# Sums of two weight matrices made by copying and accumulating DMAs instead of on VectorE

## The chip, the cores and the metric

The kernel runs on one core of a Trainium2 chip. The metric is device time in microseconds (us). The core has TensorE (PE in the profile; PEld is its weight load), VectorE (DVE), ScalarE (ACT), GpSimd (POOL) and SyncE (SP, which here only issues DMAs; its rows are written SPq). The profile counts the packets of all DMA queues on one set of 16 DMA engines; the busy share that it gives for them sums the packets' times, so it can pass 1. The granted clock is the share of full speed that the chip allowed PE. Each kernel was timed against the kernel before on the same chip.

## The reference, cut to what matters

```
x = A_x                                     # 2048 x 1024, bf16
g = sigmoid((x * gate_w).sum(-1))
a = attention(x @ wqkv) @ wo                # sliding window of 8, dilation 2, 32 heads
b = (gelu(x @ w_gate) * (x @ w_up)) @ w_down   # 1024 -> 3584 -> 1024
return g * a + (1 - g) * b
```

The last products of both branches, `... @ wo` (1024 x 1024) and `... @ w_down` (3584 x 1024), run in one accumulation, which the text below calls the down products.

## The kernel before: the parts that matter

The big products are done with seven block products in place of eight, which need sums of weight blocks. For the down products these are four sums T1 to T4 of the blocks B11, B12, B21, B22 of w_down and of wo. The sums are the same for all four chunks of 512 rows of x, so the kernel makes them once, keeps them in DRAM (`ddram`, `odram`) and loads them for every chunk.

The kernel is emitted by a small planner. Streams of operations are merged by planned time, and each engine gets its instructions in that order. What the planner believes of a DMA is this:

```python
# Weave._emit
if op.eng in ("SP", "POOL"):
    nbytes, issue = op.cost
    self.clk[op.eng] = t + issue
    self.pipe = max(self.pipe, t) + nbytes / self.RATE      # RATE = 340e3 bytes per us
    op.end = self.pipe + 2.2
```

Every engine executes strictly in the order that the planner chose. If a DMA takes longer than planned, what stands behind a wait for it on that engine is late too.

The sums before the change: SyncE loads blocks of the weights, VectorE subtracts, GpSimd stores.

```python
def preps():
    for i0 in range(0, NPREP, 2):                 # 9 groups
        ...
        f0 = dve(t, lambda: V(out=fo[:, 0], in0=b12, in1=b11, op=ALU.subtract), [("prep", i0)], lag=1.0)
        ...  # fo2 = b22 - b12,  fo1 = b22 - fo0,  fo3 = b21 - fo1
        for f in range(4):
            o = Op("POOL", (n * P * NW * 2, 0.8),
                   lambda f=f: nc.gpsimd.dma_start(out=dd[:, f, r0:r0 + n, :], in_=fo[:, f]), [last], ...)
            yield o
```

The first FFN (`ffn(0)`) has sums too, of the gate and up weights. VectorE makes them in a ring of 20 buffers, and GpSimd stores them for the second FFN. A ring buffer comes free when the matmuls have read it and its store has landed:

```python
# wforms: 56 stores
yield Op("POOL", (P * GR * 2, 0.6),
         lambda b=b, f=f: nc.gpsimd.dma_start(out=fdram[b][:, f * GR:(f + 1) * GR],
                                              in_=ring[:, held[("w", 0, b, f)], :]),
         [("w", 0, b, f)], key=("ws", b, f))
# ffn, after the last matmul that reads the sum
ring_give(("w", sup, b, form), o, w.done[("ws", b, form)])
```

SyncE loads the weight blocks into that ring. In the same queue, beside blocks 9 to 12, it loads the other half of x with transposing DMAs, in four groups of four:

```python
for b in range(2, NBLK):
    yield from load_block(0, b)
    if b >= XB:                                   # XB = 9
        for c, k0 in ((2, 0), (2, 4), (3, 0), (3, 4))[b - XB:b - XB + 1]:
            yield from list(load_x(c, []))[k0:k0 + 4]
```

Of the kernel before, what the change touches and what calls it, by code (L numbers as in the profile page):

```python
# [14 lines left out]
P = 128  # L15
# [15 lines left out]
class Op:  # L31


    def __init__(self, eng, cost, fn, deps=(), key=None, table=None, pre=None, lag=0.0, tail=0.08, kind=None):
        self.eng, self.cost, self.fn, self.deps, self.key = eng, cost, fn, deps, key
        self.table, self.pre, self.lag, self.tail = table, pre, lag, tail
        self.kind = kind
        self.end = None


class Weave:
# [42 lines left out]
    def _emit(self, op, t):  # L84
        cost = op.cost
        if op.eng == "ACT" and op.table is not None and op.table != self.table:
            self.table = op.table
            cost += 1.29
# [3 lines that stand above are left out]
            self.pipe = max(self.pipe, t) + nbytes / self.RATE  # L92
            op.end = self.pipe + 2.2
        else:
            self.clk[op.eng] = t + cost
            op.end = t + cost + op.tail
        instructions = self.nc.cur_bb.bb.instructions
        n0 = len(instructions)
        op.fn()
        for ins in self.nc.cur_bb.bb.instructions[n0:]:  # L100
            eng = getattr(ins, "engine", None)
            if eng is None or not getattr(ins, "name", None) or type(ins).__name__.startswith("BassTile"):
                continue
            prev = self.last.get(eng)
            if prev is not None:
                self.tc.add_manual_dep(ins, prev, mybir.DependencyInfo(mybir.DependencyClass.NoSync,
                                                                      mybir.DependencyReason.DATA),
                                       reason="engine order")
            self.last[eng] = ins.name
            self.names.append((ins.name, len(self.log)))  # L110
        if op.key is not None:
            self.done[op.key] = op
        self.log.append((op.eng, t, op.end, op.key, op.fn.__qualname__.split(".")[2], op.cost))
# [23 lines left out]
def kernel(  # L137
# [156 lines left out]
    w.pipe = 6.0  # L294

    vbuf = hT[:, :, 0:NT, :].rearrange("p k f n -> p k (f n)")
    NPREP = FH + NTH
    def stage(i):
        f0 = 8 + 4 * i
        return hT[:, :, f0:f0 + 4, :].rearrange("p (a b) f s -> p a b (f s)", b=2)  # L300

    def qkv_src(which, k0, n):
        return A_wqkv[k0 * P:(k0 + n) * P, which * D:(which + 1) * D].rearrange("(k p) n -> p k n", p=P)

# [5 lines left out]
    def load_x(c, deps):  # L310
        deps = deps + ([[("acct", 1)], [("att", 0)]][c - 2] if c > 1 else [])
        for kt in range(KT):
            yield Op("SP", (P * SC * 2, 1.6), lambda kt=kt: nc.sync.dma_start_transpose(
                out=xT(c, kt), in_=x[c * SC:(c + 1) * SC, kt * P:(kt + 1) * P]), deps, key=("x", c, kt))

    def load_prep(i0):
        n = min(2, NPREP - i0)
        kind, src, nr = ("d", B_w_down, FH) if i0 < FH else ("o", A_wo, NTH)
        r0 = i0 if kind == "d" else i0 - FH
        si = i0 % 5  # L320

        def fn():
            st = stage(si)
            for h, r in ((0, r0), (1, nr + r0)):
                if kind == "d":
                    v = src[r * P:(r + n) * P, :].rearrange("(k p) (h n) -> p k h n", p=P, h=2)
                else:
                    v = AP(src.tensor, src.offset + r * D, [[NT * D, P], [D, n], [NW, 2], [1, NW]])
                for k in range(n):
                    nc.sync.dma_start(out=st[:, 2 * h + k], in_=v[:, k])  # L330
        return Op("SP", (4 * n * P * NW * 2, 2.0 * n), fn, [("preps", i0 - 6)] if i0 >= 6 else [], key=("prep", i0))

    def load_block(sup, b):
        c0, c1 = b * FB * P, (b + 1) * FB * P
# [30 lines left out]

    def loads():
        yield from load_qkv(0, 0)
        yield load_prep(0)
        yield from load_qkv(0, 1)
        yield Op("SP", (KT * P * D * 2, 1.0), lambda: [nc.sync.dma_start(out=vbuf[:, hf * KH:(hf + 1) * KH],  # L370
                                                                        in_=qkv_src(2, hf * KH, KH)) for hf in range(2)],
                 [("pt", NST - 1, 1)], key=("wqkv", 0, 2))
        yield load_prep(2)
        yield from load_x(1, [])
        for i0 in (4, 6, 8, 10):
            yield load_prep(i0)
        yield from load_block(0, 0)
        yield load_prep(12)
        yield from load_block(0, 1)
        for i0 in (14, 16):  # L380
            yield load_prep(i0)
        for b in range(2, NBLK):
            yield from load_block(0, b)
            if b >= XB:
# [15 lines left out]
                yield from load_down(c0 + 1)  # L400

    def preps():
        for i0 in range(0, NPREP, 2):
            kind, r0, n = ("d", i0, min(2, FH - i0)) if i0 < FH else ("o", i0 - FH, min(2, NPREP - i0))
            st, ot = stage(i0 % 5), stage((i0 + 1) % 5)
            b11, b12, b21, b22 = st[:, 0:n, 0], st[:, 0:n, 1], st[:, 2:2 + n, 0], st[:, 2:2 + n, 1]
            fo = ot[:, :, 0:n, :]
            t = tt(n * NW)
            f0 = dve(t, lambda: V(out=fo[:, 0], in0=b12, in1=b11, op=ALU.subtract), [("prep", i0)], lag=1.0)
            yield f0  # L410
            yield dve(t, lambda: V(out=fo[:, 2], in0=b22, in1=b12, op=ALU.subtract))
            f1 = dve(t, lambda: V(out=fo[:, 1], in0=b22, in1=fo[:, 0], op=ALU.subtract), [f0])
            yield f1
            last = dve(t, lambda: V(out=fo[:, 3], in0=b21, in1=fo[:, 1], op=ALU.subtract), [f1])
            yield last
            dd = (ddram if kind == "d" else odram)[:].rearrange("f p (k n) -> p f k n", n=NW)
            for f in range(4):
                o = Op("POOL", (n * P * NW * 2, 0.8),
                       lambda f=f: nc.gpsimd.dma_start(out=dd[:, f, r0:r0 + n, :], in_=fo[:, f]), [last],
                       key=("preps", i0) if f == 3 else None)  # L420
                yield o
            if i0 + 2 == FH:
                w.done[("stored", "d")] = o
            if i0 + 2 == NPREP:
                w.done[("stored", "o")] = o

    def wforms():
        t = tt(GR)
# [280 lines left out]
    def gate(c):  # L709
# [18 lines left out]
                key=("zq", c))  # L728
        yield e
        ez = small.tile([P, SC // 32], F32, tag="ez", bufs=2, name="ez")  # L730
        omg = small.tile([P, NST], F32, tag="omg", bufs=3, name="omg")
        gates[c] = (ez, omg, zq)

    def gate_sum(c):
# [14 lines left out]
    def gate_tail(c):  # L749
        ez, omg, og = gates[c]  # L750

        def tail():
            nc.vector.tensor_scalar(out=og[:], in0=ez[:], scalar1=1.0, scalar2=1.0, op0=ALU.mult, op1=ALU.add)
            nc.vector.reciprocal(out=og[:], in_=og[:])
            for q in range(4):
                nc.vector.tensor_copy(out=omg[32 * q:32 * (q + 1), :],
                                      in_=og[32 * q:32 * (q + 1), :].rearrange("p (j q) -> p j q", q=4)[:, :, q])
        yield dve(1.2, tail, [("ez", c)], lag=0.6, key=("omg", c))

    accs = {}  # L760
# [202 lines left out]
    def ffn(sup, mid, early=()):  # L963
# [29 lines left out]
        for i in range(FT + 2):  # L993
# [33 lines left out]
            if 1 <= i < FT + 1:  # L1027
                f = i - 1
                o = yield from prod(Bk[f], 2, T3, f, False, [ev[f, "u2"]])
                d = [("stored", "o")] if (sup == 0 and f >= 8) else []  # L1030
                if sup and f >= FT - NT:
                    d = [("qkv", 2 * sup + 1, 0, 0)]
                ev[f, "up2"] = dve(tt(SC, True), lambda f=f: nc.vector.tensor_tensor(  # L1033
                    out=hs(f, 1), in0=v3(banks[Bk[f]][:]), in1=v3(m5[f][:]), op=ALU.add), [o, ev[f, "m5"]] + d)
                yield ev[f, "up2"]
# [27 lines left out]
    def down(c):  # L1063
# [31 lines left out]
        def forms():  # L1095
            for g in range(2):
                j2 = 2 * g + 1
                yield form(ops[g]["S1"], quarter(j2, 0), quarter(j2, 1), ALU.add, ("S1", c, g), hdone + [("ffn", sup)])
                yield form(quarter(j2, 0), ops[g]["A11"], quarter(j2, 0), ALU.subtract, ("S3", c, g))
            for g in range(2):  # L1100
                yield form(ops[g]["S2"], ops[g]["S1"], ops[g]["A11"], ALU.subtract, ("S2", c, g), [("pr", c, 0, g)])
# [34 lines left out]
    def down_rest(c, ops, prod, forms, form, ev, A, Bk, Dk, m5, u2, omg):  # L1136
# [18 lines left out]
        for m in range(1, 7):  # L1155
            for g in range(2):
                j1, j2 = 2 * g, 2 * g + 1
                om1, om2 = omg[:, j1:j1 + 1], omg[:, j2:j2 + 1]
                box = []
                if m == 1:  # L1160
                    o = yield from prod(A[g], m, g, False, [ev[g, "seed"]])
                    e = act(0.6, lambda g=g, om1=om1, box=box: scaled(A[g], om1, ost_tile(box)), [o, ("omg", c)])
                    yield from evac(e, j1, 0, box)
                    bank_give(A[g], e)
                    yield form(ops[g]["S4"], ops[g]["A12"], ops[g]["S2"], ALU.subtract, ("S4", c, g), [o])
                elif m == 2:
                    Dk[g], fr = bank_take()
                    o = yield from prod(Dk[g], m, g, True, [fr])
# [14 lines left out]
                elif m == 4:  # L1183
                    o = yield from prod(Bk[g], m, g, False, [ev[g, "u2"]])
                    ev[g, "x"] = dve(0.67, lambda g=g, om2=om2, box=box: nc.vector.scalar_tensor_tensor(
                        out=ost_tile(box), in0=banks[Bk[g]][:], scalar=om2, in1=m5[g][:], op0=ALU.mult, op1=ALU.add),
                        [o, ev[g, "m5"]])
                    yield from evac(ev[g, "x"], j2, 1, box)
                elif m == 5:
                    o = yield from prod(Dk[g], m, g, False, [ev[g, "m5"]])  # L1190
                    e = dve(0.67, lambda g=g, om1=om1, box=box: nc.vector.scalar_tensor_tensor(  # L1191
                        out=ost_tile(box), in0=banks[Dk[g]][:], scalar=om1, in1=u2[g][:], op0=ALU.mult, op1=ALU.add),
                        [o, ev[g, "u2"]])
                    yield from evac(e, j1, 1, box)
                    bank_give(Dk[g], e)
# [91 lines left out]
```

## Time and profile before

| | before |
|---|---|
| median of 4 runs | 730.9 us (730.65 to 731.56) |
| PE busy, share of the span | 721.8 us, 99% |
| VectorE busy | 631.6 us, 87% |
| first FFN | about 96 to 264 us |
| last store of the down and wo sums issued | 94 us; first sum loaded at 266 us |

The first part of the page of the kernel before, busy us of each engine and instructions:

```profile
PE 721.8 (99%) x3397; PEld 356.0 (49%) x3397; DVE 631.6 (87%) x935; ACT 314.9 (43%) x532; POOL 72.0 (10%) x128
```

The kernel before by stretches of the first FFN. In all lines from the profile `ring` are the weight buffers, `lend` the chunks of x, `ps` the banks that PE writes, `hT`, `tf`, `m` and `u` intermediate results. The columns are the stretch, its length, the busy us (and instructions) of PE, PEld, DVE, ACT and POOL, PE's granted clock, the busy share of the DMA engines, and GB/s:

```profile
144.00:168.00 24.00, 24.00 (x113) 10.92 (x112) 23.33 (x32) 13.27 (x25) 4.32 (x8) 1.00 0.54 174
...
192.00:216.00 24.00, 24.00 (x113) 10.88 (x111) 23.48 (x35) 13.45 (x24) 4.32 (x8) 1.00 0.96 235
216.00:240.00 24.00, 24.00 (x112) 10.87 (x111) 22.64 (x31) 13.45 (x24) 2.16 (x4) 1.00 0.43 116
```

PE has no idle time to give. The DMA engines are about half idle, except where the transposing loads run (issued from 176 to 219 us).

GpSimd's timeline before, in that stretch (start, us, what, and in brackets the idle time before it and what ended that):

```profile
204.93 0.54 POOL L443 DMA_DIRECT2D fforms<-ring  x1 [5.26 <-DVE ring L435]
208.14 0.54 POOL L443 DMA_DIRECT2D fforms<-ring  x1 [2.67 <-DVE ring L435]
```

GpSimd waits for VectorE, and stores each sum as soon as it is there. `fforms` are the gate/up sums.

From the part on DMAs (times from issue to landing, median us) come three lines of the kernel before:

```profile
fforms<-ring POOLq DMA_DIRECT2D x56, 256.0 KB, 4.5
...
ring<-in_B_w_up_dram SPq DMA_DIRECT2D x42, 256.0 KB, 3.3
...
lend<-in_A_x_dram SPq DMA_TRANSPOSE x24, 4.6
```

### The profile page before, as it was taken

What the parts mean: (1) busy time and instruction counts of PE and PEld (TensorE: products, weight loads), DVE (VectorE), ACT (ScalarE), POOL (GpSimd) and SP (SyncE); (2) the same over time, 40 slices, a digit from 0 to 9 for tenths busy, and PEclk for the clock granted to TensorE, in tenths of its full rate; (3) what the DMA queues carried; (4) which work ended last, traced back from release to release, by engine and by line L of the source; (5) the groups of instructions that cost most, each with busy time, mean ns of one, the idle gap of its engine ahead of it and who ended that gap; (6) DMA issues with size and microseconds to landing.
All of it is one profiled execution on the core that took longest, in us unless ns stands there. A gap on an engine that the chain in (4) does not pass through costs nothing.

```text
span 729.7 us, 9971 instructions
## 1 busy us (share of the span) xinstructions
PE 721.8 (99%) x3397; PEld 356.0 (49%) x3397; DVE 631.6 (87%) x935; ACT 314.9 (43%) x532; POOL 72.0 (10%) x128
## 2 busy tenths in 40 slices
PE   8999999999999999999999998999999999999998
PEld 5666644444444444456665444444444444444443
DVE  2689999999999989999899999999999999969300
ACT  2333455558555561035652113576557654220110
POOL 2234422121210100000000001000000000001000
PEclk9999999999999999999999999999999999999999
DMA  9999965648892869943029999555455544899992
GB/s 302 333 325 363 380 200 170 187 139 212 213 227 74 280 194 326 314 162 116 29 89 300 358 302 333 165 150 155 147 159 147 156 151 145 303 304 336 323 303 104
DMA packets 151507, 163.73 MB, mean 224 GB/s; under 512 B 22944, under 2 KB 112032, under 8 KB 151456
## 3 DMA queue, kind: packets, MB, share of 16 engines
q1 hardware_dynamic: 142624, 135.30, 60.1%
q0 software_dynamic: 8544, 27.27, 10.1%
q8 instruction: 26, 0.43, 0.2%
q10 hardware_dynamic: 288, 0.52, 0.2%
q14 instruction: 25, 0.20, 0.1%
HBM read 129.50 MB, written 28.31 MB: 216 GB/s over the span
## 4 chain that ended last, share of the span: by engine, by line
PE 73%; issue 21%; DVE 2%; ACT 1%; DMA 1%; POOL 1%; POOLq 0%; ACTq 0%
PE ps L970 44%; PE ps L1117 17%; PE ps L473 11%; DVE xbuf L922 1%; POOL out_dram L1144 1%; DMA hT<-in_A_x_dram 0%; DVE xbuf L930 0%; PE ps L1212 0%; DMA out_dram<-ost 0%; DVE xbuf L935 0%; DVE ost L1191 0%; ACT ost L1152 0%; ACT L1058 0%; DVE xbuf L787 0%; PE ps L717 0%
## 5 line engine op out<-in xcount | busy, mean ns | idle before, releaser
L970 PEld LDWEIGHTS <-ring 128*128 128x128 bf16 x1568 | 153.2, 98 | 187.7 <-issue 3.5
L970 PE MATMUL ps<-lend,ring 128*128 128x512 bf16 x896 | 212.3, 379 | 2.2 <-ACT m L1024 2.1
L970 PE MATMUL ps<-tf,ring 128*128 128x512 bf16 x672 | 164.0, 379 | 0.0
L1117 PE MATMUL ps<-ring,hT 128*128 128x512 bf16 x708 | 160.7, 379 | 0.0
L1117 PEld LDWEIGHTS <-hT 128*128 128x128 bf16 x708 | 69.2, 98 | 83.3
L781 DVE TENSOR_TENSOR xbuf<-qo,lend 128x2048 bf16<-128x2048 bf16 x64 | 77.4, 1218 | 2.1 <-ACT lend L495 2.1
L922 DVE TENSOR_TENSOR xbuf<-xbuf,lend 128x2048 bf16<-128x2048 bf16 x64 | 77.4, 1218 | 0.1
L787 DVE TENSOR_TENSOR xbuf<-xbuf 128x2048 bf16<-128x2048 bf16 x56 | 68.2, 1218 | 0.2
L609 PEld LDWEIGHTS <-ring 128*128 128x128 bf16 x336 | 44.0, 131 | 28.7 <-DMA ring<-in_A_wqkv_dram 0.4
L473 PE MATMUL ps<-lend,ring 128*128 128x512 bf16 x256 | 56.3, 381 | 0.1
L1042 ACT ACTIVATE gl<-ps 128x512 bf16<-128x512 f32 x56 | 33.5, 598 | 51.5 <-PE ps L970 51.4
L999 ACT COPY ps<-ps 128x512 f32<-128x512 f32 x56 | 32.0, 571 | 54.9 <-PE ps L970 54.8
L1152 ACT ACTIVATE ost<-ps,omg 128x512 bf16<-128x512 f32 x16 | 11.0, 688 | 102.5 <-PE ps L1117 99.3
L1144 POOL DMA_DIRECT2D out_dram<-ost x24 | 13.0, 540 | 413.4 <-ACT ost L1152 319.4
L1117 PE MATMUL ps<-ring,qo 128*128 128x512 bf16 x192 | 49.3, 379 | 0.0
L473 PEld LDWEIGHTS <-ring 128*128 128x128 bf16 x256 | 36.8, 145 | 19.0 <-issue 0.7
L443 POOL DMA_DIRECT2D fforms<-ring x56 | 30.4, 544 | 132.4 <-DVE ring L435 120.6
L609 PE MATMUL ps<-lend,ring 128*128 128x512 bf16 x192 | 43.5, 379 | 0.0
L1014 DVE TENSOR_TENSOR hT<-hT,gl 128x1024 bf16<-128x1024 bf16 x56 | 38.4, 686 | 5.8 <-ACT hT L1011 4.5
L930 DVE TENSOR_TENSOR xbuf<-xbuf 128x1024 bf16<-128x1024 bf16 x64 | 41.9, 686 | 0.7
L1054 DVE TENSOR_TENSOR u<-ps,u 128x512 f32<-128x512 f32 x56 | 38.4, 686 | 4.6 <-PE ps L970 3.4
L1033 DVE TENSOR_TENSOR hT<-ps,m 128x512 bf16<-128x512 f32 x56 | 38.4, 686 | 4.0 <-PE ps L970 3.9
(106 smaller groups left out, 724.7 us busy)
## 6 DMA issues: line engine op xcount, KB each, us to landing
ring<-dforms SPq DMA_DIRECT2D x112, 256.0 KB, 4.9
ring<-in_B_w_down_dram SPq DMA_DIRECT2D x84, 256.0 KB, 4.1
ring<-in_B_w_gate_dram SPq DMA_DIRECT2D x56, 256.0 KB, 4.7
fforms<-ring POOLq DMA_DIRECT2D x56, 256.0 KB, 4.5
ring<-fforms SPq DMA_DIRECT2D x56, 256.0 KB, 3.9
ring<-in_B_w_up_dram SPq DMA_DIRECT2D x42, 256.0 KB, 3.3
ring<-in_A_wqkv_dram SPq DMA_DIRECT2D x40, 256.0 KB, 4.9
ring<-oforms SPq DMA_DIRECT2D x32, 256.0 KB, 5.6
```

The costliest lines, as they stand in the source:

```text
L473: nc.tensor.matmul(banks[bk][:], lhsT=lhsT, rhs=xT(c, kt), start=(kt == 0), stop=(kt == KT - 1))
L609: nc.tensor.matmul(banks[bk][:], lhsT=lhsT, rhs=rhs[:, kt, :], start=(start and kt == 0), stop=(kt == KH - 1), skip_group_check=True)
L781: V(out=w3(box[t]), in0=q_b, in1=k_w, op=ALU.mult)
L787: V(out=w3(box[0]), in0=w3(box[0]), in1=w3(box[t]), op=ALU.add)
L922: return dve(tt(n), taking(("p", t), lambda: V(out=w3(box["p", t]), in0=w3(box["ab"]), in1=v_w, op=ALU.mult)), [("qkv", c, 2, t), abo] + ( ...
L930: V(out=s4(t)[:, t % 2], in0=w3(box["p", t])[:, 0:4], in1=w3(box["p", t])[:, 4:8], op=ALU.add)
L970: nc.tensor.matmul(banks[bk][:], lhsT=wv[:, k, fl * P:(fl + 1) * P], rhs=rhs[:, k, :], start=(start and k == 0), stop=(k == KH - 1), skip_ ...
L1014: yield dve(tt(2 * SC), lambda f=f: nc.vector.tensor_tensor(out=hT[:, :, f, :], in0=hT[:, :, f, :], in1=gl[f][:].rearrange("p (j s) -> p j ...
L1033: ev[f, "up2"] = dve(tt(SC, True), lambda f=f: nc.vector.tensor_tensor(out=hs(f, 1), in0=v3(banks[Bk[f]][:]), in1=v3(m5[f][:]), op=ALU.add ...
L1042: nc.scalar.activation(out=gl[f][:, SC:2 * SC], in_=banks[A[f]][:], func=ACT.Gelu_apprx_tanh)
L1054: e = dve(tt(SC, True), lambda f=f: nc.vector.tensor_tensor(out=u2[f][:], in0=banks[Dk[f]][:], in1=u2[f][:], op=ALU.add), [o, ev[f, "u2"]])
L1117: nc.tensor.matmul(banks[bk][:], lhsT=l, rhs=wv[:, i, :], start=(start and k == 0), stop=(q == last and i == 1), skip_group_check=True)
```

## The change

The intent is to take the down and wo sums off VectorE, and their blocks out of SyncE's queue and SBUF. GpSimd issues DRAM-to-DRAM DMAs: a plain copy puts one block in place, and accumulating DMAs add the others. The accumulates used here add and do not subtract, so signs elsewhere are changed (T1 = B11 + B12 and so on, with other operations on the activations' side and a negated gate). wo is one group of 8 DMAs of 0.5 MB. down is two groups of 8 DMAs of 0.9 MB. Each DMA waits until the one before has landed.

```diff
-    def load_prep(i0):
-        ...                                     # 36 loads of 256 KB on SyncE's queue
     def preps():
-        for i0 in range(0, NPREP, 2):
-            ...                                 # 4 subtractions, 4 stores for each group
+        def part(kind, k0, n):
+            ...
+            return [(src(0, 0), dst(0), None), (src(1, 1), dst(2), None), (src(1, 1), dst(1), None), (src(1, 0), dst(3), None),
+                    (src(0, 1), dst(0), ALU.add), (src(0, 1), dst(2), ALU.add), (dst(0), dst(1), ALU.add),
+                    (dst(1), dst(3), ALU.add)]
+        prev = [("qkv", 0, 1, NT - 1)]
+        for kind, k0, n in [("o", 0, NTH)] + [("d", k, PK) for k in range(0, FH, PK)]:     # PK = 7
+            for src, dst, op in part(kind, k0, n):
+                def go(src=src, dst=dst, op=op):
+                    if op is None:
+                        nc.gpsimd.dma_start(out=dst, in_=src)
+                    else:
+                        nc.gpsimd.dma_start(out=dst, in_=src, accum_op=op, max_dma_last_dim=1024)
+                o = Op("POOL", (n * P * NW * 2 * (2 if op else 1), 1.0), go, prev, after=True)
                 yield o
+                prev = [o]
+            w.done[("stored", kind)] = o
...                                              # Weave._emit: after=True makes a real wait for the op before
...                                              # down(): signs, and a second, negated copy of the gate
```

More of the change, by code (lines that the diff above doesn't have):

```diff
@@ L31, with __init__ @@
 class Op:
-    def __init__(self, eng, cost, fn, deps=(), key=None, table=None, pre=None, lag=0.0, tail=0.08, kind=None):
+    def __init__(self, eng, cost, fn, deps=(), key=None, table=None, pre=None, lag=0.0, tail=0.08, kind=None, after=False):
         self.eng, self.cost, self.fn, self.deps, self.key = eng, cost, fn, deps, key
@@ L37, in __init__ @@
         self.kind = kind
+        self.after, self.ins = after, None
         self.end = None
@@ L108, in _emit @@
                                        reason="engine order")
+            if op.after and op.ins is None:
+                for d in self._deps(op):
+                    self.tc.add_manual_dep(ins, d.ins, mybir.DependencyInfo(mybir.DependencyClass.Sync,
+                                                                           mybir.DependencyReason.DATA),
+                                           reason="kept behind")
+            op.ins = ins.name
             self.last[eng] = ins.name
@@ L296 @@
     vbuf = hT[:, :, 0:NT, :].rearrange("p k f n -> p k (f n)")
-    NPREP = FH + NTH
-    def stage(i):
-        f0 = 8 + 4 * i
-        return hT[:, :, f0:f0 + 4, :].rearrange("p (a b) f s -> p a b (f s)", b=2)
+    PK = 7
     def qkv_src(which, k0, n):
@@ L314, in load_x @@
                 out=xT(c, kt), in_=x[c * SC:(c + 1) * SC, kt * P:(kt + 1) * P]), deps, key=("x", c, kt))
-    def load_prep(i0):
-        n = min(2, NPREP - i0)
-        kind, src, nr = ("d", B_w_down, FH) if i0 < FH else ("o", A_wo, NTH)
-        r0 = i0 if kind == "d" else i0 - FH
-        si = i0 % 5
-        def fn():
-            st = stage(si)
-            for h, r in ((0, r0), (1, nr + r0)):
-                if kind == "d":
-                    v = src[r * P:(r + n) * P, :].rearrange("(k p) (h n) -> p k h n", p=P, h=2)
-                else:
-                    v = AP(src.tensor, src.offset + r * D, [[NT * D, P], [D, n], [NW, 2], [1, NW]])
-                for k in range(n):
-                    nc.sync.dma_start(out=st[:, 2 * h + k], in_=v[:, k])
-        return Op("SP", (4 * n * P * NW * 2, 2.0 * n), fn, [("preps", i0 - 6)] if i0 >= 6 else [], key=("prep", i0))
     def load_block(sup, b):
@@ L367, in loads @@
         yield from load_qkv(0, 0)
-        yield load_prep(0)
         yield from load_qkv(0, 1)
@@ L372, in loads @@
                  [("pt", NST - 1, 1)], key=("wqkv", 0, 2))
-        yield load_prep(2)
         yield from load_x(1, [])
-        for i0 in (4, 6, 8, 10):
-            yield load_prep(i0)
         yield from load_block(0, 0)
-        yield load_prep(12)
         yield from load_block(0, 1)
-        for i0 in (14, 16):
-            yield load_prep(i0)
         for b in range(2, NBLK):
@@ L402, in preps, with src, dst @@
     def preps():
-        for i0 in range(0, NPREP, 2):
-            kind, r0, n = ("d", i0, min(2, FH - i0)) if i0 < FH else ("o", i0 - FH, min(2, NPREP - i0))
-            st, ot = stage(i0 % 5), stage((i0 + 1) % 5)
-            b11, b12, b21, b22 = st[:, 0:n, 0], st[:, 0:n, 1], st[:, 2:2 + n, 0], st[:, 2:2 + n, 1]
-            fo = ot[:, :, 0:n, :]
-            t = tt(n * NW)
-            f0 = dve(t, lambda: V(out=fo[:, 0], in0=b12, in1=b11, op=ALU.subtract), [("prep", i0)], lag=1.0)
-            yield f0
-            yield dve(t, lambda: V(out=fo[:, 2], in0=b22, in1=b12, op=ALU.subtract))
-            f1 = dve(t, lambda: V(out=fo[:, 1], in0=b22, in1=fo[:, 0], op=ALU.subtract), [f0])
-            yield f1
-            last = dve(t, lambda: V(out=fo[:, 3], in0=b21, in1=fo[:, 1], op=ALU.subtract), [f1])
-            yield last
-            dd = (ddram if kind == "d" else odram)[:].rearrange("f p (k n) -> p f k n", n=NW)
-            for f in range(4):
-                o = Op("POOL", (n * P * NW * 2, 0.8),
-                       lambda f=f: nc.gpsimd.dma_start(out=dd[:, f, r0:r0 + n, :], in_=fo[:, f]), [last],
-                       key=("preps", i0) if f == 3 else None)
+        def part(kind, k0, n):
+            def src(kh, nh):
+                if kind == "o":
+                    return AP(A_wo.tensor, A_wo.offset + (kh * NTH + k0) * D + nh * NW, [[NT * D, P], [D, n], [1, NW]])
+                r0 = (kh * FH + k0) * P
+                return B_w_down[r0:r0 + n * P, nh * NW:(nh + 1) * NW].rearrange("(k p) n -> p k n", p=P)
+            def dst(f):
+                return (odram if kind == "o" else ddram)[f][:, k0 * NW:(k0 + n) * NW].rearrange("p (k n) -> p k n", k=n)
+            return [(src(0, 0), dst(0), None), (src(1, 1), dst(2), None), (src(1, 1), dst(1), None), (src(1, 0), dst(3), None),
+                    (src(0, 1), dst(0), ALU.add), (src(0, 1), dst(2), ALU.add), (dst(0), dst(1), ALU.add),
+                    (dst(1), dst(3), ALU.add)]
@@ L421, in preps @@
                 yield o
-            if i0 + 2 == FH:
-                w.done[("stored", "d")] = o
-            if i0 + 2 == NPREP:
-                w.done[("stored", "o")] = o
+                prev = [o]
+            w.done[("stored", kind)] = o
     def wforms():
@@ L730, in gate @@
         ez = small.tile([P, SC // 32], F32, tag="ez", bufs=2, name="ez")
-        omg = small.tile([P, NST], F32, tag="omg", bufs=3, name="omg")
+        omg = small.tile([P, 2 * NST], F32, tag="omg", bufs=3, name="omg")
         gates[c] = (ez, omg, zq)
@@ L755, in tail @@
             for q in range(4):
-                nc.vector.tensor_copy(out=omg[32 * q:32 * (q + 1), :],
+                nc.vector.tensor_copy(out=omg[32 * q:32 * (q + 1), 0:NST],
                                       in_=og[32 * q:32 * (q + 1), :].rearrange("p (j q) -> p j q", q=4)[:, :, q])
+            nc.vector.tensor_scalar(out=omg[:, NST:2 * NST], in0=omg[:, 0:NST], scalar1=-1.0, scalar2=None, op0=ALU.mult)
         yield dve(1.2, tail, [("ez", c)], lag=0.6, key=("omg", c))
@@ L1029, in ffn @@
                 o = yield from prod(Bk[f], 2, T3, f, False, [ev[f, "u2"]])
-                d = [("stored", "o")] if (sup == 0 and f >= 8) else []
+                d = []
                 if sup and f >= FT - NT:
@@ L1097, in forms @@
                 j2 = 2 * g + 1
-                yield form(ops[g]["S1"], quarter(j2, 0), quarter(j2, 1), ALU.add, ("S1", c, g), hdone + [("ffn", sup)])
+                yield form(ops[g]["S1"], quarter(j2, 0), quarter(j2, 1), ALU.subtract, ("S1", c, g), hdone + [("ffn", sup)])
                 yield form(quarter(j2, 0), ops[g]["A11"], quarter(j2, 0), ALU.subtract, ("S3", c, g))
@@ L1157, in down_rest @@
                 j1, j2 = 2 * g, 2 * g + 1
-                om1, om2 = omg[:, j1:j1 + 1], omg[:, j2:j2 + 1]
+                om1, om2, nom2 = omg[:, j1:j1 + 1], omg[:, j2:j2 + 1], omg[:, NST + j2:NST + j2 + 1]
                 box = []
@@ L1164, in down_rest @@
                     bank_give(A[g], e)
-                    yield form(ops[g]["S4"], ops[g]["A12"], ops[g]["S2"], ALU.subtract, ("S4", c, g), [o])
+                    yield form(ops[g]["S4"], ops[g]["A12"], ops[g]["S2"], ALU.add, ("S4", c, g), [o])
                 elif m == 2:
@@ L1185, in down_rest @@
                     ev[g, "x"] = dve(0.67, lambda g=g, om2=om2, box=box: nc.vector.scalar_tensor_tensor(
-                        out=ost_tile(box), in0=banks[Bk[g]][:], scalar=om2, in1=m5[g][:], op0=ALU.mult, op1=ALU.add),
+                        out=ost_tile(box), in0=banks[Bk[g]][:], scalar=nom2, in1=m5[g][:], op0=ALU.mult, op1=ALU.add),
                         [o, ev[g, "m5"]])
@@ L1191, in down_rest @@
                     e = dve(0.67, lambda g=g, om1=om1, box=box: nc.vector.scalar_tensor_tensor(
-                        out=ost_tile(box), in0=banks[Dk[g]][:], scalar=om1, in1=u2[g][:], op0=ALU.mult, op1=ALU.add),
+                        out=ost_tile(box), in0=banks[Dk[g]][:], scalar=om1, in1=u2[g][:], op0=ALU.mult, op1=ALU.subtract),
                         [o, ev[g, "u2"]])
```

## The prediction

> **What bounds the kernel now.** TensorE. The page's busy table has PE at 721.8 of 729.7 us (99%); the table by stretches shows it busy in 12.00 of every 12 us from 60 to 168 us. Idle PE is about 2 us at the start, 2 at 440-480 and 4 at the end. The clock is 1.00. No matmul is added or removed, so the change cannot gain 2%.
>
> **Removed.** 36 VectorE subtractions of about 0.69 us (25 us of VectorE's 632), 36 weight loads of 256 KB on SyncE's queue and 36 GpSimd stores of 256 KB, done by 94 us (timeline of GpSimd). The DMA engines, at share 1.0-1.1 from 60 to 96 us, are relieved. None of this is on PE's chain. Expected gain: 0 to 2 us.
>
> **Added.** 24 DRAM-to-DRAM DMAs, each kept behind the one before: for wo eight of 0.5 MB, for down sixteen of 0.9 MB, half of each accumulating. The Trainium skill ("Collectives: The Full Stack", the part on the bandwidth ceiling) says that a reduce in the DMA reads two sources per write and so runs at about half the copy's rate; no trace here shows an accumulate yet. Estimates from this trace: a 256 KB store lands 4.5 us after issue, a 1 MB load 11.4 us on busy engines, a 1 MB SBUF copy 10.0. I take 5.5 and 7 us for a wo copy and accumulate, 7.5 and 10 for down: 50 + 140 = 190 us. The first may start near 36 us (K of the first chunk), so the last ends near 226 us.
>
> **What lies on the critical path.** Two deadlines.
> 1. The first down product that needs a sum loads from 266 us. About 40 us of slack.
> 2. GpSimd works in order, and a DMA that waits for its predecessor holds up the 56 stores of the gate/up sums (67 to 246 us). Those stores free ring buffers. A store is issued 24 to 35 us before its sum's last matmul (block 3: stores 109-116 us, matmuls end near 144), so GpSimd may lag by about 30 us before the ring runs short; then loads and VectorE sums stop, and PE with them. The planner charges about 5 us a copy and 8 an accumulate of down weights; if they cost 7.5 and 10, the lag builds to 20-40 us: just around the slack. DMA share in 96-180 us is only 0.52-0.62, so bandwidth suffices; latency in series is the risk, most of all at 180-216 us (share 0.9-1.0, the transposing loads).
>
> So most likely nothing is lost; one chance in three is for a stall of PE in the first FFN, of 15 to 100 us, if an accumulate costs over about 13 us.
>
> **Prediction:** 732 us, 8 in 10 between 728 and 775. Faster by over 2%: 0.01; within 2%: 0.65; slower: 0.34.
>
> **What would show it.** Right: PE stays full through the first FFN; VectorE's busy time falls by 25 us to about 607 while the span does not move; the last accumulate lands before 235 us; accumulates land near 10 us after issue, copies near 7.5. Wrong: GpSimd's waits show long waits for its own DMAs, stores of the gate/up sums lag over 30 us, PE gaps between 130 and 260 us that end on ring loads or VectorE sums, or a gap at the first down product.
>
> **What would make it wrong.** An accumulate far slower than half rate (1 KB pieces, contention with SyncE's loads); slow descriptor making for 900 rows on GpSimd; a changed order on VectorE or GpSimd that delays an evacuation.

## The result

The changed kernel takes 752.36 us (median of 4 runs, 750.5 to 752.57) beside 730.9 us before. The ratio is 1.0287, with a 95% interval of 1.0269 to 1.0304. It is slower by 2.9%. Here and below, a ratio is the mean time of one kernel's fast runs over that of the other's of the same rounds, so it is not quite the ratio of the medians quoted. The time lies within the predicted range, but far from the estimate of 732 us.

The first part of the page after the change:

```profile
PE 728.1 (97%) x3397; PEld 357.2 (48%) x3397; DVE 609.4 (81%) x903; ACT 316.2 (42%) x533; POOL 75.8 (10%) x116
```

VectorE was relieved of 22.2 us (631.6 less 609.4). PE's busy time grew by 6.3 us for the same 3397 matmuls, and the span by 20.9 us. So PE also stood idle for 14.6 us more.

The same stretches after the change, and the two next to them where most is lost:

```profile
144.00:168.00 24.00, 21.47 (x100) 9.69 (x99) 18.66 (x27) 11.85 (x21) 7.95 (x11) 1.00 1.01 263
...
192.00:216.00 24.00, 20.67 (x97) 9.31 (x96) 19.22 (x26) 10.80 (x20) 7.94 (x10) 1.00 1.22 227
216.00:240.00 24.00, 19.11 (x79) 8.01 (x78) 13.30 (x16) 9.72 (x18) 6.11 (x9) 0.93 1.16 268
240.00:264.00 24.00, 18.44 (x75) 7.89 (x75) 20.41 (x42) 12.79 (x21) 4.34 (x8) 0.86 0.84 229
```

The loss is all in the first FFN, while the chain of DMAs runs and just after its end. VectorE is idle there as well, so its speed is not what holds PE. The DMA engines are at a share of 1.0 to 1.2 up to 240 us.

GpSimd's timeline after the change, late in the chain:

```profile
198.41 1.71 POOL L402 DMA_DIRECT2D dforms<-in_B_w_down_dram  x1 [10.76 <-DMA dforms<-in_B_w_down_dram]
199.42 2.95 POOL L424 DMA_DIRECT2D fforms<-ring  x4
209.99 1.75 POOL L402 DMA_DIRECT2D dforms<-dforms  x1 [7.62 <-DMA dforms<-in_B_w_down_dram]
210.99 2.98 POOL L424 DMA_DIRECT2D fforms<-ring  x4
223.78 1.74 POOL L402 DMA_DIRECT2D dforms<-dforms  x1 [9.80 <-DMA dforms<-dforms]
224.78 4.56 POOL L424 DMA_DIRECT2D fforms<-ring  x7
```

GpSimd now waits for its own DMAs, not for VectorE. The stores go out in bunches of four and seven behind each wait, so they had been ready before. The planner, which can print its own log, had the last accumulate at 191.7 us; it was issued at 223.8 us, so GpSimd ran 32 us behind its plan. Not all of that is GpSimd's own: by the same log, the sums that VectorE made at 223 to 228 us were 11 to 14 us late themselves. Before the stalls, at 144 to 154 us, the chain was already 17 to 20 us late and VectorE's sums were on their plan.

The same DMA lines after the change, with the new ones:

```profile
fforms<-ring POOLq DMA_DIRECT2D x56, 256.0 KB, 8.6
...
ring<-in_B_w_up_dram SPq DMA_DIRECT2D x42, 256.0 KB, 5.8
...
dforms<-in_B_w_down_dram POOLq DMA_DIRECT2D x12, 896.0 KB, 7.5
...
dforms<-dforms POOLq DMA_DIRECT2D x4, 896.0 KB, 10.4
...
lend<-in_A_x_dram SPq DMA_TRANSPOSE x24, 8.0
```

The time from one DMA's start to the next in GpSimd's timeline is on average 7.5 us after a down copy (8 of them), 11.7 us after a down accumulate (7), 4.2 us after a wo copy (4) and 7.1 us after a wo accumulate (4). The stores of the sums and the loads of weights land later than before, and the transposing loads take nearly twice as long.

Two lines of PE's timeline after the change, the first stall-free and the second behind the longest gap, each of eight matmuls:

```profile
237.37 1.89 PE L952 MATMUL ps<-lend,ring 128*128 128x512 bf16 x8
245.56 3.57 PE L952 MATMUL ps<-tf,ring 128*128 128x512 bf16 x8 [6.30 <-DVE hT L1015]
```

After a gap of 6.3 us the same work took 3.57 us, not 1.89. The Trainium skill ("TensorE: Matmul & The Clock Gate", part 1) says that the clock halves after an idle window of about 3.4 us. After this gap and one of 4.1 us the trace agrees; a gap of 2.5 us was followed by slow matmuls too, and one of 3.3 us was not (see the closing list). The slow matmuls behind the three gaps are 5.9 us longer than at full clock, which is nearly all of the 6.3 us by which PE's busy time grew: these stalls are paid a second time.

### The profile page after: what moved, and what is told of

It is laid out like the page before. It is cut to its first block, busy times and chain, and to the rows that moved or that the text cites. A ratio compares the mean times of both kernels' runs of the same rounds, so it can differ in the third digit from the quotient of the medians.

```text
span 750.6 us, 9822 instructions
## 1 busy us (share of the span) xinstructions
PE 728.1 (97%) x3397; PEld 357.2 (48%) x3397; DVE 609.4 (81%) x903; ACT 316.2 (42%) x533; POOL 75.8 (10%) x116
## 4 chain that ended last, share of the span: by engine, by line
PE 86%; DMA 6%; issue 4%; SPq 2%; DVE 1%; POOL 1%; ACT 1%; POOLq 0%; DVEq 0%
PE ps L952 35%; PE ps L1099 29%; PE ps L454 11%; PE ps L590 10%; DMA ring<-in_B_w_up_dram 3%; SPq L316 2%; DMA fforms<-ring 1%; DMA ring<-in_B_w_gate_dram 1%; DMA dforms<-in_B_w_down_dram 1%; DMA hT<-in_A_x_dram 0%; PE ps L1194 0%; POOL fforms L424 0%; PE ps L698 0%; DVE ring L416 0%; DVE hT L1015 0%
## 5 line engine op out<-in xcount | busy, mean ns | idle before, releaser
L952 PE MATMUL ps<-tf,ring 128*128 128x512 bf16 x672 | 166.4, 383 | 12.2 <-DVE hT L1015 12.2
L416 DVE TENSOR_TENSOR ring<-ring 128x1024 bf16<-128x1024 bf16 x56 | 37.3, 686 | 28.0 <-DMA ring<-in_B_w_up_dram 15.6
L1040 ACT ACTIVATE gl<-u 128x512 bf16<-128x512 f32 x56 | 35.5, 633 | 33.2 <-DVE u L1036 33.1
```

The lines of the kernel that those rows point to most:

```text
L416: nc.vector.tensor_tensor(out=g, in0=ring[:, held[("w", 0, b, x_)], :], in1=ring[:, held[("w", 0, b, y_)], :], op=op)
L952: nc.tensor.matmul(banks[bk][:], lhsT=wv[:, k, fl * P:(fl + 1) * P], rhs=rhs[:, k, :], start=(start and k == 0), stop=(k == KH - 1), skip_ ...
L1040: ev[f, "g2"] = act(0.54, lambda f=f: nc.scalar.activation(out=gl[f][:, 0:SC], in_=u2[f][:], func=ACT.Gelu_apprx_tanh), [e], table="gelu")
```

## The experiments

Three theories were held against each other in turn.

- **Lag (L).** GpSimd, held by its own DMAs, issues the stores late. Ring buffers come free late, and SyncE's loads with them.
- **Contention (C, later A).** The accumulates share the DMA engines with SyncE's loads, and these land late.
- **Two causes (T).** The lag is one. The other is that the accumulates slow the transposing loads, behind which SyncE's in-order queue holds the weight loads.

Twelve kernels were run, one of them (`before_x_late`) a control.

### Four first runs

`stores_act` sends the gate/up stores through ScalarE's DMA queue.

```diff
-                    yield Op("POOL", (P * GR * 2, 0.6),
-                             lambda b=b, f=f: nc.gpsimd.dma_start(
+                    yield Op("ACT", 0.1,
+                             lambda b=b, f=f: nc.scalar.dma_start(
...
-                             [("w", 0, b, f)], key=("ws", b, f))
+                             [("w", 0, b, f)], key=("ws", b, f), tail=4.5)
```

> The 56 stores of the gate/up sums go to ScalarE's DMA queue instead of GpSimd's; the 24 chained DMAs stay. Theory L (lag: GpSimd, held by its own DMAs, issues these stores late, so ring buffers come free late): the stores land about 5 us after issue, PE is full from 120 to 265 us, 729 to 735 us. Rival C (contention: the accumulating DMAs share the DMA engines with SyncE's weight loads and transposing loads, which land late): loads of the up weights still land in about 6 us or more and PE still stalls, 745 to 752 us.

Measured: 748.59 us beside 732.29, ratio 1.0218 (1.0191 to 1.0246). PE now loses nothing from 96 to 168 us, where the change lost 3.3 us, but from 168 to 264 us it loses 15.8 us, where the change lost 13.8. The time is in the range of rival C; the run of the last four that repeats this edit shows why it can't decide between the two.

`plan_true` leaves every DMA as it is, and only lets the planner charge the chain what the trace showed. The order of the other engines' work changes with the plan.

```diff
-            op.end = self.pipe + 2.2
+            op.end = self.pipe + 2.2 + op.lag
...
-                o = Op("POOL", ..., go, prev, after=True)
+                o = Op("POOL", ..., go, prev, after=True, lag=(3.5 if op else 2.0) if kind == "d" else (1.5 if op else 0.3))
```

> The planner charges each chained DMA what the trace showed (2.0 us more for a down copy, 3.5 us more for a down accumulate, 0.3 and 1.5 for wo), so that it puts the stores ahead of a DMA that would hold them; the same DMAs and bytes. Theory L: GpSimd no longer runs behind its plan, stores land early, 729 to 736 us. Rival C: the traffic is the same, so 744 to 752 us.

Measured: 745.84 us, ratio 1.0191 (1.0151 to 1.0231). The chain is now on its plan (the last accumulate 2.2 us late, not 32), and no load of SyncE waits for a store any more, but PE still stands idle for 11.2 us from 168 to 264 us (96 less 22.71, 21.19, 21.86 and 19.06), at a granted clock of 0.93 and 0.86 in the last two of these four stretches. The time is in the range that rival C gave. The lag is not the only cause. The chain of waits of this run, in its last part:

```profile
200.81 12.76 DMA ring<-in_B_w_up_dram
...
218.95 10.64 DMA ring<-in_B_w_gate_dram
...
236.71 10.20 DMA ring<-in_B_w_gate_dram
```

VectorE's sums wait for loads of the weights that take 10 to 13 us.

`copies_only` turns every accumulate into a plain copy. Its output is wrong, which doesn't matter for the time.

```diff
-                        nc.gpsimd.dma_start(out=dst, in_=src, accum_op=op, max_dma_last_dim=1024)
+                        nc.gpsimd.dma_start(out=dst, in_=src)
```

> Wrong result on purpose: each accumulating DMA becomes a plain copy of the same bytes to the same place, all waits and the order of issue kept. The period of a down accumulate (about 11.5 us now) should fall to that of a copy (about 7.5). Both theories expect a recovery to 729 to 737 us, L because GpSimd then lags its plan by under 10 us; if the time stays above 745 us both are wrong and the number of DMAs or the order is the cause.

Measured: 734.14 us, ratio 1.0028 (1.0007 to 1.0049). The same 24 DMAs, each still waiting for the one before, cost next to nothing without the adding (about 2 us; PE loses 3.1 us from 192 to 216 us). So neither the number of DMAs, nor the waiting in order as such, nor the changed order of the other engines is by itself the cause; the accumulates are, by their length or by their traffic (the edit also drops the cutting into pieces, `max_dma_last_dim`). The last DMA starts at 193.4 us, on its plan.

`early` starts the chain at once.

```diff
-        prev = [("qkv", 0, 1, NT - 1)]
+        prev = []
```

> The chain starts at once, not after K of the first chunk (some 30 us earlier). The plan moves with it, so by theory L the lag behind the plan still builds to some 25 to 30 us, but it ends at about 210 us instead of 234: 738 to 748 us. By rival C the accumulates now end before the transposing loads of 176 to 236 us are through, so most of the collision stays away only at the end: 735 to 745 us. The start may suffer: the loads of the first qkv weights share the engines with the wo copies, at most 2 us.

Measured: 746.85 us, ratio 1.0208 (1.0184 to 1.0232). PE is full to 192 us and loses 15.4 us from 192 to 240 us, where the transposing loads stand. The range of L held, and that of C was just missed. By itself this tells little; it fits with the transposing loads being part of the matter.

In the three of these runs that accumulate, PE is full up to 168 us (in `early` up to 192 us) and stalls while the transposing loads run. That led to theory T.

### Four runs on the transposing loads

`x_plain` replaces the 16 transposing loads by plain loads of as many bytes (a wrong result), with the chain as in the change. `x_plain_plan` adds the true charge of `plan_true`.

```diff
                 yield Op("SP", (P * SC * 2, 1.6), lambda kt=kt: nc.sync.dma_start_transpose(
-                out=xT(c, kt), in_=x[c * SC:(c + 1) * SC, kt * P:(kt + 1) * P]), deps, key=("x", c, kt))
+                out=xT(c, kt), in_=x[c * SC:(c + 1) * SC, kt * P:(kt + 1) * P]) if c < 2 else nc.sync.dma_start(
+                out=xT(c, kt), in_=x[c * SC + kt * 32:c * SC + kt * 32 + P, 0:SC]), deps, key=("x", c, kt))
```

> Wrong result on purpose: the 16 transposing loads of x (chunks 2 and 3, issued from 176 to 240 us) become plain loads of the same bytes; all else, the chain of 24 DMAs too, is that of the change. Theory T (two causes: GpSimd runs behind its plan, and the accumulates slow the transposing loads, behind which SyncE's in-order queue holds the weight loads): PE still loses some 3 to 6 us before 168 us, but little after, 734 to 742 us. Rival A (the accumulates slow every load, transposing or not): PE still stalls from 190 to 264 us, 745 to 752 us.

> Wrong result on purpose: as x_plain, and the planner charges the DMAs what they cost (as in plan_true). Theory T: both causes are out, PE full from 96 to 264 us, 729 to 734 us. Rival A: as plan_true, 742 to 748 us.

`x_late` keeps the transposing loads and the right result, but puts them behind the last weight block. `x_late_plan` adds the true charge.

```diff
         for b in range(2, NBLK):
             yield from load_block(0, b)
-            if b >= XB:
-                for c, k0 in ((2, 0), (2, 4), (3, 0), (3, 4))[b - XB:b - XB + 1]:
-                    yield from list(load_x(c, []))[k0:k0 + 4]
+        for c in (2, 3):
+            yield from load_x(c, [])
```

> Right result: the same 16 transposing loads stand behind the last weight block in SyncE's queue (planned from 226 us), where only the last accumulate can meet them; the plan is else unchanged. Theory T: as x_plain, 733 to 743 us, unless the first loads of the down products, now behind 16 transposing loads, come late for 260 us. Rival A: 745 us or more.

> Right result: x_late and plan_true together. The chain ends at about 244 us by plan, so the last two or three accumulates meet the transposing loads again. Theory T: 731 to 738 us. Rival A: 742 us or more.

Measured, medians in us, with the kernel before at 730.81 in these rounds and at 732.29 in those of `plan_true`:

| transposing loads | planner's charge as in the change | true charge |
|---|---|---|
| beside blocks 9 to 12 | 752.36 (the change) | 745.84 (`plan_true`) |
| replaced by plain loads | 750.54 (`x_plain`) | 733.57 (`x_plain_plan`) |
| behind the last block | 744.77 (`x_late`) | 734.19 (`x_late_plan`) |

The ratios are 1.0267 (1.0252 to 1.0282) for `x_plain`, 1.0031 (1.0014 to 1.0048) for `x_plain_plan`, 1.0198 (1.0176 to 1.0219) for `x_late` and 1.0042 (1.0028 to 1.0057) for `x_late_plan`.

`x_plain` alone would have spoken for rival A, in whose range it came. Rival A falls as the main cause with the two runs of the true charge: with both causes out, the accumulates still run among the weight loads, and only 3 us remain, where A expected 742 us or more. Theory T was right in its two causes and wrong in taking them to add up. `x_plain` was expected at 734 to 742 us and came at 750.5, and `x_late` missed its range too. Either cause alone keeps most of the loss; only the removal of both removes it.

The lag at work is read from what SyncE's queue waits for. One line of that view for the change, then for `x_plain`, then for `x_late` (total us, times, longest):

```profile
SPq L328 <- DMA fforms<-ring: 17.0, 8, 5.4
```

```profile
SPq L329 <- DMA fforms<-ring: 32.3, 10, 9.9
```

```profile
SPq L328 <- DMA fforms<-ring: 48.5, 14, 10.6
```

Loads of weight blocks wait for stores of the sums to land. The less the transposing loads hold SyncE, the more the late stores do: whichever is out of the way, the other is met (this is read from the three lines; no run shows it by itself). In the kernel before, in `plan_true`, `x_plain_plan` and `x_late_plan` there is no such line at all.

The other cause is read from SyncE's timeline: the four transposing loads of one group take this long to issue, in the kernel before and then in `plan_true`:

```profile
200.30 6.36 SPq L313 DMA_TRANSPOSE lend<-in_A_x_dram  x4
```

```profile
204.97 11.05 SPq L316 DMA_TRANSPOSE lend<-in_A_x_dram  x4
```

The weight loads stand behind them. Summed over the four groups it is 25.8 us before (6.96, 5.77, 6.36, 6.73) and 37.0 us in `plan_true` (7.21, 8.94, 11.05, 9.77), of which the trace puts only 3.4 us down to waits for other engines. The 16 plain loads of `x_plain_plan` take 21.8 us.

The hold in the queue is not the whole of this cause. In `copies_only` the 16 transposing loads take 32.4 us to issue (9.13, 9.93, 6.66, 6.68; copies ran beside the first two groups), so the chain's copies slow them as well, and yet that run loses little. What differs is how long the weight loads behind them then take to land. From 168 to 252 us, in the kernel before, the change, `plan_true`, `x_late_plan` and `copies_only`:

```profile
DMA to landing us min/median/max: 2.7/4.2/5.8
DMA to landing us min/median/max: 4.5/9.6/14.4
DMA to landing us min/median/max: 4.7/10.7/13.3
DMA to landing us min/median/max: 4.2/9.6/10.8
DMA to landing us min/median/max: 3.0/6.1/15.4
```

Slow landing without the hold (`x_late_plan`) costs 3 us, and the hold with faster landing (`copies_only`) 2 us; `plan_true` has both and loses 13.5 us. These runs differ in more than one thing, so this suggests, and does not prove, that it takes both parts.

GpSimd's timeline of `x_late_plan`, at the place shown of the change:

```profile
206.10 1.75 POOL L401 DMA_DIRECT2D dforms<-in_B_w_down_dram  x1 [3.65 <-DMA dforms<-in_B_w_down_dram]
208.84 0.60 POOL L423 DMA_DIRECT2D fforms<-ring  x1 [1.00 <-DMA ring<-in_B_w_gate_dram]
211.19 0.54 POOL L423 DMA_DIRECT2D fforms<-ring  x1 [1.74 <-DVE ring L415]
...
216.94 1.77 POOL L401 DMA_DIRECT2D dforms<-dforms  x1 [2.81 <-DMA dforms<-in_B_w_down_dram]
```

The accumulates take as long as in the change (10.8 and 11.3 us from start to start here). The stores are in the gaps instead of behind them, each issued when VectorE has made its sum.

### Four last runs

`stores_act_x_late` takes the stores off GpSimd in another way (the edits of `stores_act` and `x_late` together), with the planner's charge as in the change.

> Right result: the stores of the gate/up sums on ScalarE's queue (stores_act) and the 16 transposing loads behind the last weight block (x_late); the planner charges the chain as the change does. Theory T says the lag hurts only through these stores, so taking them off GpSimd must do as much as the true charge did: 731 to 737 us, beside 734.2 of x_late_plan. If what helped in plan_true was another effect of the changed plan (the order of VectorE and ScalarE), this stays at 740 us or more.

Measured: 749.44 us beside 731.79, ratio 1.0235 (1.0212 to 1.0257): a miss, and it looks like a refutation of the lag. The trace says otherwise. The stretches of `x_late` and of this run, from 144 us:

```profile
144.00:168.00 24.00, 19.47 (x89) 8.77 (x90) 16.05 (x23) 11.05 (x20) 8.11 (x11) 1.00 0.99 260
```

```profile
144.00:168.00 24.00, 24.00 (x113) 10.90 (x112) 22.90 (x36) 13.31 (x24) 2.65 (x2) 1.00 1.06 251
...
192.00:216.00 24.00, 24.00 (x113) 10.88 (x111) 23.55 (x31) 13.26 (x25) 3.40 (x2) 1.00 0.95 260
...
240.00:264.00 24.00, 16.30 (x59) 6.50 (x59) 10.88 (x25) 11.90 (x21) 0.00 (x0) 0.76 1.04 205
```

With the stores away from GpSimd PE is full from 144 to 216 us (and in its timeline up to 232.8), where `x_late` and the change had lost several microseconds. The whole loss comes after that, from something new, in ScalarE's timeline of this run:

```profile
238.53 1.28 ACT L860 ACT_TABLE_LOAD   x1 [9.34 <-DMA lend<-in_A_x_dram]
...
250.63 0.58 ACT L1005 COPY m<-ps 128x512 f32<-128x512 f32 x1 [7.17 <-DMA lend<-in_A_x_dram]
```

ScalarE, which also empties PE's banks, stood 9.3 and 7.2 us before work that follows a store, and the trace puts the end of these waits down to the transposing loads. The listing of the program shows that a store on this queue waits for one or two semaphores of SyncE's DMAs, beside VectorE's. So the edit put a new wait of its own on the critical path. This run supports the lag up to 232 us and can't be used after that. The listing also says why the stores carry those waits: the DMAs of SyncE and ScalarE take turns on eight semaphores, and each of the 56 stores waits for the DMA before it on its own semaphore, which is a weight load of SyncE for 19 of them and a transposing load for 5. In `stores_act` it is 23 and 6, so the same must be held against the total time of that run.

`early_x_late_plan` is `x_late_plan` with `prev = []`, the candidate for the best version of the change.

> Right result, the candidate for the best version: x_late_plan with the chain started at once. The chain ends near 221 us by plan, before the transposing loads begin at 226. Theory T: 730 to 733 us, thus level with the kernel before; the stall of about 2.6 us between 192 and 240 us of x_late_plan shrinks only if it came from the overlap with the transposing loads.

Measured with five rounds: 729.08 us (728.63 to 729.91) beside 731.79, ratio 0.996 (0.9944 to 0.9975). This is just under the expected 730 to 733 us. PE is full from 192 to 264 us. The result is right. The change is harmless in this form.

`before_x_late` is the control: the kernel before with the edit of `x_late` alone.

> Control: the kernel before with the transposing loads moved behind the last weight block. They collide with nothing there and hold up nothing, so it should be 730 to 732 us. A gain of over 2 us would mean that x_late helps by itself.

Measured: 728.58 us (728.33 to 728.77), ratio 0.9954 (0.9937 to 0.9971). The later transposing loads gain 3 us on their own, slightly more than allowed for. In the kernel before PE was busy 77.93 of 80 us from 400 to 480 us, and here 80.00 of 80. So the 729.08 us of the best changed version are due to `x_late`, not to the accumulates: against this control the relief of VectorE is worth nothing (0.5 us slower by the medians).

`x_late_plan_copies` is `x_late_plan` with copies in place of accumulates. Its output is wrong, which doesn't matter for the time.

> Wrong result on purpose: x_late_plan with each accumulate made a plain copy. Both causes are out and the chain is lighter; if the 3.4 us that x_late_plan still lacks are the accumulates' hold on the plain weight loads, this is 730 to 732 us; if they are another cost of the change, it stays near 734 us.

Measured: 730.55 us (728.17 to 733.35), ratio 0.9982 (0.9957 to 1.0008), beside 734.19 of `x_late_plan` in rounds whose kernel before was at 730.81. With neither cause left, the accumulates still cost about 4 us more than copies (1.0042 less 0.9982, of 731; some 2 to 7 us by the two intervals, and the two runs were on different chips). In `x_late_plan` the weight loads of 168 to 252 us land after 9.6 us in the median; in the kernel before it is 4.2 us. The ring is mostly, not wholly, deep enough for that.

## Why the prediction was right, and where it was not

The measured 752.36 us lies between 728 and 775, so the range held. It held by its breadth, since it took in the stall to which the prediction gave one chance in three. The estimate of 732 us and the 0.65 for "within 2%" were on the wrong side of a limit that the prediction itself had named.

- **PE bounds the kernel, so nothing can be gained.** Right. VectorE's busy time fell by 22.2 us (25 predicted), and even the version without stalls is no faster than its control.
- **The cost of the chain.** Right in size. Predicted were 5.5 and 7 us for a wo copy and accumulate, and 7.5 and 10 us for down. Measured were 4.2, 7.1, 7.5 and 11.7 us. The end, predicted at 226 us, was near 234 us (223.8 plus 10.4 to landing). The prediction drew on the Trainium skill ("Collectives: The Full Stack", the bandwidth ceiling), where a reduce runs at half of a copy's rate. Here the whole DMA took 1.6 times as long as a copy (11.7 by 7.5), fixed parts included.
- **The lag of GpSimd.** Right in mechanism and size: 20 to 40 us predicted, 32 us measured at the last accumulate, some 20 us of it before PE's larger stalls. `plan_true` and the SyncE waits show that it matters.
- **"GpSimd may lag by about 30 us before the ring runs short".** This is the step that failed, with its consequence that a stall needs an accumulate of over about 13 us. The figure was the time from one store to the last matmul of its own sum. The stall came with accumulates of 11.7 us. PE had lost 3.3 us by 168 us, 2.5 of them in a gap at 165 us, when GpSimd was only 17 to 20 us behind its plan (the DMAs of the chain planned at 126.5, 134.2 and 142.8 us started at 143.8, 154.1 and 161.5). Before that gap SyncE had waited 3.6 us for a store to land, and the weight load behind it then took about 9 us, not 4.2, so the slack was shortened from the other side as well. With the stores off GpSimd (`stores_act`) or ahead of the chain (`plan_true`) nothing was lost up to 168 us.
- **"DMA share in 96-180 us is only 0.52-0.62, so bandwidth suffices".** Wrong. The share rose to 1.0 and above, the median landing of SyncE's weight loads from 168 to 252 us from 4.2 to 9.6 us. By itself this costs little: `x_late_plan` has the same 9.6 us and takes 734.19 us. Together with the transposing loads it was the second cause. The prediction had named the transposing loads at 180 to 216 us, but as a danger to the chain. The danger was the other way: the chain slowed them, they held up the weight loads, and these landed late. `plan_true` against `x_plain_plan` prices this at about 12 us when the lag is out (745.84 less 733.57).
- **The clock.** Not foreseen. Of the 20.9 us of span, 6.3 us are matmuls at a lower clock after stalls.

What stays open: how the loss in the unchanged plan divides between the two causes, which overlap in time; that they hide one another in the same queue is argued from the waits, not shown by a run. The true charge changes the planned order of every engine, not of GpSimd alone, and the run meant to separate the two (`stores_act_x_late`) did so only up to 232 us; that the true charge helps by removing the lag rests on that stretch, on `stores_act` up to 168 us and on SyncE's waits. No run changed the size of the accumulate's pieces, so whether the two reads or the pieces make it slow is open too.

## What to carry to other kernels

A DMA that an engine waits for in order is not free because the engine is idle: ask what stands behind it in the same queue, what that frees, and by how much the real time exceeds what the plan allows. When the removal of one suspected cause changes nothing, remove it together with the next one before acquitting it, since two causes can each be enough. Moving work from an engine that is not the bottleneck gains nothing, while the traffic that replaces it can hit whatever shares the DMA engines, and a control with the side edit alone shows who earned the gain.

## What the Trainium skill lacked or had wrong

- "DMA: Bandwidth & Descriptors" says that accumulating DMAs are issued from GpSimd but gives no time for one. Here a 896 KB DRAM-to-DRAM accumulate took 10.3 to 13.8 us from start to start, and a copy of the same size 6.0 to 8.9 us.
- The same page (Issuing engines are not separate DMA queues) says that all queues run on the same 16 engines and interleave; the trace agrees. It lacks what that costs a reader of another queue: beside the chain, 256 KB loads landed after 9.6 us in the median, not 4.2, and a group of four transposing loads took up to 12.4 us to issue, not 5.8 to 7.0.
- "Collectives: The Full Stack" (the bandwidth ceiling) puts a reduce at half of a copy's rate. Here the time of a whole DMA was 1.6 times that of a copy; no run separated the fixed part.
- "TensorE: Matmul & The Clock Gate" (part 1) names an idle window of about 3.4 us before the clock halves. In the changed kernel gaps of 4.1 and 6.3 us agree with it, but a gap of 2.5 us was already followed by slow matmuls (eight in 3.09 us, not 1.89), and a gap of 3.3 us elsewhere was not, so here the length of the gap alone did not decide.
